# A decayed linear attention and a two-layer MLP in one kernel: the order of the work rewritten, attention in whole chunks on raw scores, its outputs token-major and turned by DMA

## The chip, the core and the metric

One NeuronCore of a Trainium2 chip. The metric is the device time of one execution in microseconds (us), the median of three runs. The profile beside it is of one execution; its span runs from the first to the last recorded instruction.

Names of the engines: PE is the matrix engine (its weight loads are a row of their own, PEld), DVE the vector engine, ACT the scalar engine, POOL the GpSimd engine, SP the sync engine, which here only issues DMAs. Each engine takes its instructions in the order in which the program wrote them for it.

## What is computed

```python
B, H, S, D = 4, 8, 768, 64; block = 64
for b in range(S // block):                          # q, k, v, per head h with decay lam[h]
    intra = (q_b k_b^T * lam^(i-j) for i >= j) v_b
    inter = (q_b * lam^(i+1)) state
    out_b = intra + inter
    state = lam^block * state + (k_b * lam^(block-1-j))^T v_b
x = out as [B * S, H * D]                            # 3072 tokens x 512
h = x @ w_in                                         # 512 x 2048
g = h * tanh(softplus(h))                            # Mish
return g @ w_out                                     # 2048 x 512, f32
```

Both kernels take chunks of 128 positions instead of blocks of 64, which gives the same sums, and compute in float16 with float32 accumulation.

## The kernel before, in words

The sequence is cut into six groups n = 0 to 5. A group is 128 positions of all four batches, so four chunks (n, b) of 128 tokens by 8 heads; its x has 512 tokens. The work of a group has three parts.

**Attention**, before: half a chunk (four heads, two pairs of heads) at a time. `att_a` (L306, once for every half) makes q and k feature-major. For group 1 PE does it, for groups 2 to 5 a DMA transpose on SP's queue (`turn`, L263 to L268). DVE multiplies q by a table of decays (`qT`, L318 or L341), k has been multiplied by its decay before (`scale_k`, L256). Each pair's two heads are copied apart into a zero-padded tile (`kz`, L322 on DVE or L344 on ACT), so that one matmul of 128 rows gives one head's scores. `att_s` (L353) makes four 128x128 score matmuls, and DVE multiplies them by the causal mask (`sb`, L362). `att_o` (L365) adds the state's part and the scores' part, feature-major, so that the result is x as the first layer wants it (L375, L379), and ACT copies it out (`xt`, L382). `att_kv` (L276) and `att_w` (L290) make the new state (matmuls `pv` L283, `raw` L298 on DVE, `w` L299 on POOL).

**First layer**: 16 units of 128 features, each four matmuls of 512 columns into a PSUM bank `ph` and one Mish on ACT into `hsg` (L420, L434).

**Second layer**: for group 0 plain, 64 matmuls of 512 columns (`po`, L442). For groups 1 to 5 as the seven products of a 2x2 block scheme (`fast_unit` L593, `product` L518), each 16 matmuls of 256 columns; DVE makes the sums of the operands (`gsum` L498 per group, `tsum` L479 once) and the combinations of the results.

The order is written out by hand: at group n PE runs the 16 units and the 14 half products of group n, and the attention pieces of group n+1 are let in after given units (`room`, L661 to L667). Loads of q, k and v are issued from POOL's queue, 128 KB each, weights before them (L124 to L143). Outputs leave from SP's and ACT's queues.

Of the kernel before, what the change touches and what calls it, by code (L numbers as in the profile page):

```python
# [20 lines left out]
def kernel(  # L21
# [10 lines left out]
    nc = tc.nc  # L32
# [10 lines left out]
    NVB = 8  # L43
    NKB = 4
    NT = 2
# [3 lines left out]
    loads = ctx.enter_context(tc.tile_pool(name="loads", bufs=NVB))  # L49
    work = ctx.enter_context(tc.tile_pool(name="work", bufs=2))  # L50
    ps = ctx.enter_context(tc.tile_pool(name="ps", bufs=1, space=bass.MemoryType.PSUM))


    kn = [None] * (NG * B)
    qn = [None] * (NG * B)

    vz = [const.tile([128, H, 2 * D], F16, name=f"vz{i}") for i in range(NVB)]

    def chunk_rows(t, i):
        n, b = divmod(i, B)  # L60
        return t[b, :, n * C : (n + 1) * C, :].rearrange("h p c -> p h c")

    def load_k(i):
        if i == 0:
            kn[i] = const.tile([128, H, D], F32, name="kn0")
            nc.sync.dma_start(out=kn[i], in_=chunk_rows(k, i))
            return
        kn[i] = loads.tile([128, H, D], F16, name="kn", tag="kn")
        nc.gpsimd.dma_start(out=kn[i], in_=chunk_rows(k, i))  # L69

    def load_q(i):
        if i == 0:
            qn[i] = const.tile([128, H, D], F32, name="qn0")
            nc.scalar.dma_start(out=qn[i], in_=chunk_rows(q, i))
            return
        qn[i] = loads.tile([128, H, D], F16, name="qn", tag="qn")
        nc.gpsimd.dma_start(out=qn[i], in_=chunk_rows(q, i))  # L77

    def load_v(i):
        nc.gpsimd.dma_start(out=vz[i % NVB][:, :, 0:D], in_=chunk_rows(v, i))  # L80

    WS = 4

    cuts = (0, 128, 256, DF // WS)
    win0 = [const.tile([128, NKC, b_ - a_], F16, name=f"win0{a_}") for a_, b_ in zip(cuts, cuts[1:])]
    win = [None] + [const.tile([128, NKC, DF // WS], F16, name=f"win{s}") for s in range(1, WS)]
    wout = [const.tile([128, NKI // WS, DMO], F16, name=f"wout{s}") for s in range(WS)]

    def load_win(s):
        w = DF // WS  # L90
        if s == 0:
            for t, a_, b_ in zip(win0, cuts, cuts[1:]):
                nc.gpsimd.dma_start(
                    out=t, in_=moe_w_in[:, a_:b_].rearrange("(k p) f -> p k f", p=128))
            return
        nc.gpsimd.dma_start(
            out=win[s],
            in_=moe_w_in[:, s * w : (s + 1) * w].rearrange("(k p) f -> p k f", p=128),
        )

    def load_wout(s):
        w = DF // WS
        nc.gpsimd.dma_start(
            out=wout[s],
            in_=moe_w_out[s * w : (s + 1) * w, :].rearrange("(k p) f -> p k f", p=128),
        )

    def load_chunk(i):
        load_k(i)
        load_q(i)  # L110
        load_v(i)
# [4 lines left out]
    rel = const.tile([128, C], F32, name="rel")  # L116
    maskT = const.tile([128, C], F32, name="maskT")
    gone = const.tile([128, C], F32, name="gone")
    ei = const.tile([128, C], F32, name="ei")
    k0 = const.tile([128, H, D], F16, name="k0")  # L120
    q0 = const.tile([128, H, D], F16, name="q0")
    ek = const.tile([128, 1], F32, name="ek")

    load_k(0)  # L124
    load_q(0)
    nc.scalar.preload_act_table_set("natural_log_exp_and_others")
    load_k(1)
    nc.gpsimd.iota(rel, pattern=[[1, C]], base=0, channel_multiplier=-1,
                   allow_small_or_imprecise_dtypes=True)
    for f, i in ((load_q, 1), (load_v, 0), (load_k, 2), (load_q, 2)):  # L130
        f(i)
    nc.gpsimd.iota(ek, pattern=[[0, 1]], base=MID, channel_multiplier=-1,
                   allow_small_or_imprecise_dtypes=True)
    for f, i in ((load_v, 1), (load_k, 3), (load_q, 3), (load_v, 2), (load_v, 3)):
        f(i)
    for s in range(WS):
        load_win(s)
    for s in range(WS):
        load_wout(s)
    nc.gpsimd.iota(ei, pattern=[[1, C]], base=-MID, channel_multiplier=0,  # L140
                   allow_small_or_imprecise_dtypes=True)
    for i in range(B, 2 * B):
        load_chunk(i)  # L143
# [609 lines left out]
```

## Time and profile before

| | |
|---|---|
| median of three runs | 219.91 us (219.43 to 221.17) |
| profiled execution, span | 217.4 us |
| PE busy | 204.8 us, 94% |
| DVE busy | 146.1 us, 67% |
| POOL busy | 116.6 us, 54% |
| ACT busy | 101.3 us, 47% |
| granted PE clock | full, in every slice |
| HBM | 27.26 MB read, 6.29 MB written |

PE's busy time in the page ends a matmul where its result is out; the next one starts well before that, so that the time a matmul keeps PE from the next one is read from the distance between starts. The medians of the runs lie 2.5 us over the span: what lies around the recorded instructions.

### The profile page before, as it was taken

Reading aid. Unit: us, or ns where it says so; the run is one execution under the profiler, and the core shown is the slowest. Engines: PE = TensorE matmul, PEld = TensorE weight load, DVE = VectorE, ACT = ScalarE, POOL = GpSimd, SP = SyncE. Lnnn points to the kernel's source line nnn. Section 1 sums busy time; section 2 is a strip of 40 time slices with the busy share of each in tenths; the row PEclk is TensorE's granted clock in tenths of the full one; section 3 lists DMA queues with packets and bytes.
Section 4 is the critical chain, followed back from the end, with each engine's and each line's share of the span. In section 5 each row is a group of like instructions: output and inputs, shape, how many; then the busy total and the mean of one; then the engine's idle time right before and its main releaser. Section 6 shows DMA issues by size and latency. Waiting matters only on the chain.

```text
span 217.4 us, 4272 instructions
## 1 busy us (share of the span) xinstructions
PE 204.8 (94%) x1672; PEld 136.6 (63%) x1672; DVE 146.1 (67%) x309; ACT 101.3 (47%) x190; POOL 116.6 (54%) x139
## 2 busy tenths in 40 slices
PE   7899999999999799999979999979999999999993
PEld 2465544576545587745669845669845699644893
DVE  6667561877669999339999419999439987213433
ACT  5465566567665231166522176623166632266410
POOL 7996334998988768808757908757700002000020
PEclk9999999999999999999999999999999999999999
DMA  9999999999999999975999965999985201300014
GB/s 133 141 158 198 203 203 175 175 152 125 150 149 104 100 75 121 163 152 70 104 71 113 142 160 74 119 75 71 151 168 100 48 3 48 130 18 0 0 59 137
DMA packets 103766, 24.66 MB, mean 113 GB/s; under 512 B 93890, under 2 KB 103234, under 8 KB 103746
## 3 DMA queue, kind: packets, MB, share of 16 engines
q0 software_dynamic: 78080, 13.37, 80.3%
q1 hardware_dynamic: 22688, 8.39, 17.8%
q10 hardware_dynamic: 2978, 2.62, 4.0%
q8 instruction: 13, 0.21, 0.4%
q14 instruction: 7, 0.06, 0.1%
HBM read 27.26 MB, written 6.29 MB: 154 GB/s over the span
## 4 chain that ended last, share of the span: by engine, by line
PE 63%; DVE 20%; POOL 5%; issue 4%; DMA 4%; ACT 1%; ACTq 0%; POOLq 0%; DVEq 0%
PE ph L420 26%; PE z L525 10%; PE po L442 6%; PE y L525 6%; PE x L525 5%; DVE qT L318 5%; DVE kz L322 4%; DVE sb L362 4%; DVE gsum L498 4%; DMA win<-in_moe_w_in_dram 4%; PE pO L379 3%; DVE raw L298 3%; PE pS L358 2%; PE fin L525 2%; POOL vz L80 2%
## 5 line engine op out<-in xcount | busy, mean ns | idle before, releaser
L420 PE MATMUL ph<-xt,win 128*128 128x512 f16 (+2 forms) x404 | 89.6, 368 | 0.5 <-ACT hsg L434 0.2
L434 ACT ACTIVATE hsg<-ph 128x512 f16<-128x512 f32 x96 | 57.0, 597 | 45.6 <-PE ph L420 45.5
L420 PEld LDWEIGHTS <-win 128*128 128x128 f16 x404 | 37.0, 98 | 35.1 <-issue 0.6
L299 POOL TENSOR_TENSOR w<-raw,lbm 128x256 f16<-128x256 f32 x32 | 25.2, 791 | 29.0 <-DVE raw L298 28.9
L578 POOL TENSOR_TENSOR u<-u,p 128x512 f32<-128x512 f32 x5 | 6.5, 1293 | 52.0 <-DVE u L576 52.0
L525 PEld LDWEIGHTS <-gsum 128*128 128x128 f16 x336 | 30.8, 98 | 3.5 <-issue 0.5
L362 DVE TENSOR_TENSOR sb<-pS,maskT 128x512 f16<-128x512 f32 x40 | 27.2, 683 | 2.0 <-PE pS L358 1.9
L382 ACT ACTIVATE xt<-pO 128x256 f16<-128x256 f32 x40 | 15.2, 382 | 27.4 <-PE pO L379 27.2
L318 DVE TENSOR_TENSOR qT<-qraw,lq 128x256 f16<-128x256 f16 x32 | 19.1, 598 | 10.3 <-DMA qraw<-qn 10.3
L525 PEld LDWEIGHTS <-hsg 128*128 128x128 f16 x240 | 22.7, 98 | 2.5
L69 POOL DMA_DIRECT2D kn<-in_k_dram x23 | 21.4, 932 | 4.5 <-DMA win<-in_moe_w_in_dram 1.7
L80 POOL DMA_DIRECT2D vz<-in_v_dram x24 | 21.7, 906 | 3.3 <-DMA wout<-in_moe_w_out_dram 1.7
L77 POOL DMA_DIRECT2D qn<-in_q_dram x23 | 20.7, 898 | 5.1 <-DMA wout<-in_moe_w_out_dram 3.3
L498 DVE TENSOR_TENSOR gsum<-hsg 128x1024 f16<-128x1024 f16 x20 | 14.5, 725 | 12.9 <-ACT hsg L434 12.9
L322 DVE COPY kz<-kraw 64x256 f16<-64x256 f16 x64 | 19.9, 311 | 1.9 <-DMA kraw<-ktil 0.9
L379 PE MATMUL pO<-sb,vz 128*128 128x128 f16 x160 | 17.3, 219 | 3.6 <-DVE sb L362 3.2
L525 PE MATMUL z<-tsum,gsum 128*128 128x256 f16 x160 | 20.4, 272 | 0.2
L525 PE MATMUL x<-wout,hsg 128*128 128x256 f16 x160 | 20.1, 273 | 0.0
L358 PE MATMUL pS<-qT,kz 128*128 128x128 f16 x160 | 16.6, 220 | 1.8 <-DVE kz L322 1.6
L358 PEld LDWEIGHTS <-kz 128*128 128x128 f16 x160 | 11.8, 98 | 7.8 <-DVE kz L322 3.0
L298 DVE TENSOR_TENSOR raw<-pv,w 128x256 f32<-128x256 f32 x32 | 13.5, 422 | 4.1 <-PE pv L283 3.4
L379 PEld LDWEIGHTS <-vz 128*128 128x128 f16 x160 | 12.6, 98 | 5.7 <-issue 4.9
(89 smaller groups left out, 242.8 us busy)
## 6 DMA issues: line engine op xcount, KB each, us to landing
out_dram<-osum SPq DMA_DIRECT2D x14, 256.0 KB, 3.2
vz<-in_v_dram POOLq DMA_DIRECT2D x24, 128.0 KB, 4.7
kn<-in_k_dram POOLq DMA_DIRECT2D x23, 128.0 KB, 4.4
qn<-in_q_dram POOLq DMA_DIRECT2D x23, 128.0 KB, 4.6
wout<-in_moe_w_out_dram POOLq DMA_DIRECT2D x4, 512.0 KB, 16.5
win<-in_moe_w_in_dram POOLq DMA_DIRECT2D x3, 512.0 KB, 10.1
out_dram<-osum ACTq DMA_DIRECT2D x5, 256.0 KB, 4.0
out_dram<-osb ACTq DMA_DIRECT2D x4, 256.0 KB, 5.5
```

The costliest lines, as they stand in the source:

```text
L69: nc.gpsimd.dma_start(out=kn[i], in_=chunk_rows(k, i))
L80: nc.gpsimd.dma_start(out=vz[i % NVB][:, :, 0:D], in_=chunk_rows(v, i))
L299: nc.gpsimd.tensor_tensor(out=w_new, in0=raw, in1=lb, op=ALU.mult)
L318: nc.vector.tensor_tensor(out=s.qT, in0=qraw[i][:, 2 * hf : 2 * hf + 2, :], in1=lqh, op=ALU.mult)
L322: nc.vector.tensor_copy(s.kz[rs, :, hp, :], kraw[i][rs, 2 * hf : 2 * hf + 2, :])
L358: nc.tensor.matmul(psS[:, 2 * p + hp, :], s.kz[:, p, hp, :], s.qT[:, p, :], start=True, stop=True,)
L362: nc.vector.tensor_tensor(out=s.sb, in0=psS, in1=bc(maskT, 1, 4), op=ALU.mult)
L379: nc.tensor.matmul(psO[:, p, :], vf[:, o : o + 128], s.sb[:, 2 * p + hp, :], start=False, stop=(hp == 1))
L420: nc.tensor.matmul(ph_t[ni][:, lo:hi], win0[min(ni, 2)][:, kc, max(ni - 2, 0) * 128 : max(ni - 2, 0) * 128 + 128] if ni < w else win[ni // ...
L434: nc.scalar.activation(hsg[n][:, ni, :], ph_t.pop(ni), AF.Mish)
L498: nc.vector.tensor_tensor(out=gsum[n, i][:, ks, :], in0=a, in1=b, op=op)
L525: nc.tensor.matmul(t, lhs(kk, b), rhs(kk, c, c + w), start=(fresh and kk == 0 and (alone or i == 0)), stop=(kk == HK - 1), skip_group_chec ...
```

## The change

The kernel is written anew around the same parts. What it does:

- **Scores**: a whole chunk at a time. q and k are transposed raw and not scaled. A head's scores come from 64 rows of both, without the zero-padded copies: 8 matmuls of 64 rows by 128 columns, even heads into bank `be`, odd ones into `bo`. DVE multiplies each bank by the mask that carries the key's decay (`sb`, L247).
- **Outputs**: token-major. Four matmuls q by state (128 columns) and eight `sb` by v (64 columns) into bank `bz` (L263, L268). DVE multiplies by the query's decay (`xn`, L271), and a DMA transpose on SP writes `xt` (L274). Two chunks of group 1 are turned by PE instead (`later`, L280).
- **State**: one step a chunk instead of two (L289, L297, L298).
- **Transposes of q and k**: for groups 2 to 5 in pairs of chunks, 128x1024 (L230); groups 0 and 1 on PE.
- **Second layer**: group 0 also by the seven products, in the order 1, 2, 6, 5, 7, 3, 4 through two banks G and H. After product 1 ACT copies G to H (L440), product 2 goes on in G, 6 and 7 and 4 in H.
- **Order**: group 0's first layer holds group 1's attention; group 1's first layer follows in halves of 256 columns (`two_units`) with the rest of it and a part of group 2's; then group 0's second layer with the rest of group 2's attention; then, for n = 1 to 4, group n's second layer, group n+1's first layer and group n+2's attention in turns; at the end group 5's second layer by itself.
- **Loads** of q, k, v in pairs of chunks (256 KB); weights between them, the second layer's after the first pair of group 2. All outputs leave from SP.

```diff
-    NVB = 8
-    NKB = 4
-    NT = 2
...
+    def turn_dma(n, bp):
+        for t, to in (("k", kT), ("q", qT)):
+            tile_ = work.tile([128, 2 * JP, C], F16, name=f"{t}T", tag=f"{t}T", bufs=2)
+            nc.sync.dma_start_transpose(out=tile_, in_=pairs[t, n, bp].rearrange("p h c -> p (h c)"))
...
+    def decay_k(n, b, eng):
+        kd[n, b] = work.tile([128, H, D], F16, name="kd", tag="kd", bufs=3)
+        eng.tensor_tensor(out=kd[n, b], in0=kn[n, b], in1=bc(lk, 2, D), op=ALU.mult)
+    def scores(n, b):
+        p_ = [bank(t, [JP, C]) for t in "eo"]
+        for j in range(JP):
+            for t in range(2):
+                rs = slice(64 * t, 64 * t + 64)
+                nc.tensor.matmul(p_[t][:, j, :], kT[n, b][rs, j, :], qT[n, b][rs, j, :],
+                                 start=True, stop=True)
+        for t in range(2):
+            sb[n, b, t] = work.tile([128, JP, C], F16, name="sb", tag="sb", bufs=4)
+            nc.vector.tensor_tensor(out=sb[n, b, t], in0=p_[t], in1=dm[:, t], op=ALU.mult)
...
+    def outputs(n, b, turn=None):
+        po = bank("z", [H, D])
...
+        for j in range(JP):
+            for t in range(2):
+                nc.tensor.matmul(po[:, 2 * j + t, :], sb[n, b, t][:, j, :], vn[n, b][:, 2 * j + t, 0:D],
+                                 start=False, stop=True, skip_group_check=True)
+        xn = work.tile([128, H, D], F16, name="xn", tag="xn", bufs=2)
+        nc.vector.tensor_tensor(out=xn, in0=po, in1=bc(lq, 2, D), op=ALU.mult)
+        dst = x_tile(n)[:, :, b * C : (b + 1) * C]
+        if turn is None:
+            nc.sync.dma_start_transpose(out=dst, in_=xn.rearrange("p h c -> p (h c)"))
+            return None
...
+    def state(n, b, tag, eng):
+        pv = bank(tag, [JP, 128])
+        for j in range(JP):
+            nc.tensor.matmul(
+                pv[:, j, :].rearrange("p (a e) -> p a e", a=2), flat(kd[n, b], j),
+                vn[n, b][:, 2 * j : 2 * j + 2, 0:D], start=True, stop=True)
...
+            raw = work.tile([128, JP, 128], F32, name="raw", tag="raw", bufs=2)
+            nc.vector.tensor_tensor(out=raw, in0=pv, in1=wst[n, b], op=ALU.add)
+            eng.tensor_tensor(out=w_new, in0=raw, in1=lbm, op=ALU.mult)
+        wst[n + 1, b] = w_new
...
+    def two_units(n, ni, r):
+        t = bank(next_bank(), [2, HC])
+        cs = slice(r * HC, r * HC + HC)
+        for u in range(2):
+            for kc in range(NKC):
+                m = (ni + u) % 4 * 128
+                nc.tensor.matmul(
+                    t[:, u, :], win[ni // 4][:, kc, m : m + 128], xt[n][:, kc, cs],
+                    start=(u == 0 and kc == 0), stop=(kc == NKC - 1), skip_group_check=True)
+        nc.scalar.activation(h_tile(n)[:, ni : ni + 2, cs], t, AF.Mish)
...
-    def mm2_unit(n, b, part):
...
-    def fast_unit(n, step, blk):
...
+        def half(p, blk):
+            if blk == 0 and p in (1, 5, 3):
+                m.g = bank("G", [2, HN])
+            t = m.g if p in (1, 2, 5, 3) else m.h
+            product(n, p, t[:, blk, :], blk, p in (1, 5, 3) and blk == 0)
+            if blk == 0:
+                return
+            if p == 1:
+                m.h = bank("H", [2, HN])
+                nc.scalar.activation(m.h, m.g, AF.Copy)
+            elif p == 2:
+                o = osum()
+                nc.scalar.activation(o, m.g, AF.Copy)
+                store(n, 0, 0, o)
+            elif p == 5:
+                m.p5 = work.tile([128, 2, HN], F32, name="r5", tag="r5", bufs=1)
+                nc.scalar.activation(m.p5, m.g, AF.Copy)
+                m.u4 = work.tile([128, 2, HN], F32, name="u4", tag="u4", bufs=1)
+                nc.vector.tensor_tensor(out=m.u4, in0=m.h, in1=m.p5, op=ALU.add)
+            elif p == 7:
+                o = osum()
+                nc.vector.tensor_tensor(out=o, in0=m.h, in1=m.p5, op=ALU.add)
+                store(n, 1, 1, o)
+            elif p == 3:
+                o = osum()
+                nc.vector.tensor_tensor(out=o, in0=m.g, in1=m.u4, op=ALU.add)
+                store(n, 0, 1, o)
+            elif p == 4:
+                o = osum()
+                nc.scalar.activation(o, m.h, AF.Copy)
+                store(n, 1, 0, o)
+        return [(lambda p=p, blk=blk: half(p, blk)) for p in (1, 2, 6, 5, 7, 3, 4) for blk in range(2)]
...
-    for n in range(NG):
-        units = [(mm1_unit, (n, ni)) for ni in range(NKI)]
...
+    first_units(2)
+    first_state(0, "e")
+    first_units(3)
+    first_state(1, "o")
+    for bp in range(2):
+        for t in "kqv":
+            load_pair(t, 2, bp)
+        if bp == 0:
+            for s in range(WS):
+                load_wout(s)
+    first_units(8)
+    first_state(2, "e")
+    first_units(9)
+    first_state(3, "o")
+    first_units(10, 11)
+    turn1(0)
+    decay_k(1, 0, nc.vector)
+    sums(0, 0, 2, 0)
+    first_units(4)
+    scores(1, 0)
+    turn1(1)
+    first_units(5)
+    decay_k(1, 1, nc.vector)
+    first_units(6)
+    outputs(1, 0)
+    state(1, 0, "e", nc.vector)
+    first_units(7)
+    scores(1, 1)
+    sums(0, 0, 1, 3)
+    first_units(12, 13)
+    outputs(1, 1)
+    state(1, 1, "e", nc.vector)
+    turn1(2)
+    first_units(14)
+    scores(1, 2)
+    turn1(3)
+    first_units(15)
+    decay_k(1, 2, nc.vector)
...
+    halves = dense2(0)
...
+    h(1)
+    attended(2, 1)
+    for t, bp in (("k", 0), ("q", 0), ("v", 0)):
+        load_pair(t, 3, bp)
+    for i in range(2):
+        weight_sum(3, i)
+    h(3)
+    attend(2, 2, nc.gpsimd)
+    h(3)
+    attended(2, 2)
+    sums(1, 0, 0, 1)
+    h(1)
+    attend(2, 3, nc.gpsimd)
+    turn_dma(3, 0)
+    h(3)
+    attended(2, 3)
+    for t, bp in (("k", 1), ("q", 1), ("v", 1)):
+        load_pair(t, 3, bp)
+    sums(1, 0, 2, 3)
+    h(3)
...
+    for n in range(1, NG - 1):
...
+        h(3)
+        u(0)
+        s_(0)
+        if m < NG:
+            turn_dma(m, 1)
+        sums(n, 1, 0, 1)
+        u(1)
+        h(1)
+        u(2)
+        o_(0)
+        fetch(("k", 0), ("q", 0))
+        u(3)
+        h(1)
+        u(8)
+        s_(1)
+        sums(n, 1, 2, 3)
+        h(1)
+        u(9, 10)
+        o_(1)
+        fetch(("v", 0), ("k", 1))
+        h(1)
+        u(11)
+        h(1)
+        u(4)
+        s_(2)
+        if m + 1 < NG:
+            turn_dma(m + 1, 0)
+        u(5)
+        h(1)
+        u(6)
+        o_(2)
+        fetch(("q", 1), ("v", 1))
+        h(1)
+        sums(n + 1, 0, 0, 1)
+        h(1)
+        u(7)
+        h(1)
+        u(12)
+        s_(3)
+        sums(n + 1, 0, 2, 3)
+        h(1)
+        u(13)
+        h(1)
+        o_(3)
+        u(14, 15)
+    sums(NG - 1, 1, 2, 0, 1, 3)
+    dense2_alone(NG - 1)
```

In the order's lines `h(m)` writes the next m half products of the second layer, `u` a unit of group n+1, `s_(b)` a chunk's decayed k and scores, `o_(b)` its outputs and state (`attend` and `attended` do the same for group 2), `sums` operand sums on DVE, `fetch` loads.

How this moves instructions on two engines. First DVE during group 1's attention; before, this stood under group 0's second layer. `raw` and `w` are the state, `qT` and `kd` the operands, `sb` the masked scores.

```order
L479 TENSOR_TENSOR tsum_201<-wout_85,wout_83 128x1024
L341 TENSOR_TENSOR qT<-pq,lq 128x256
L298 TENSOR_TENSOR raw<-pv,w_184 128x256
L341 TENSOR_TENSOR qT<-pq,lq 128x256
L298 TENSOR_TENSOR raw<-pv,w_186 128x256
L362 TENSOR_TENSOR sb<-pS,maskT 128x512
```

With the change DVE has the following there, under group 0's first layer.

```order
L225 COPY qT<-bz 128x512
L236 TENSOR_TENSOR kd<-kn,lk 128x512
L384 TENSOR_TENSOR gsum_474<-hsg 128x1024
L384 TENSOR_TENSOR gsum_476<-hsg 128x1024
L247 TENSOR_TENSOR sb<-be,dm 128x512
L247 TENSOR_TENSOR sb<-bo,dm 128x512
L225 COPY qT<-bz 128x512
L236 TENSOR_TENSOR kd<-kn,lk 128x512
L271 TENSOR_TENSOR xn<-bz,lq 128x512
L297 TENSOR_TENSOR raw<-be,w_383 128x512
L298 TENSOR_TENSOR w_383<-raw,lbm 128x512
```

The operand sums of group 0's second layer, the decay of k and the state's product with `lbm` (before on POOL) now stand in this queue ahead of and between the steps that PE's attention waits for.

Second, ACT at the start of a group's second layer. Before (group 2), products 1 and 7 are copied out of two banks that are written in turns, with the attention's copies between.

```order
L568 ACTIVATE p_1693<-x 128x512
L382 ACTIVATE xt<-pO 128x2x128
L570 ACTIVATE p_1729<-z 128x512
L382 ACTIVATE xt<-pO 128x2x128
L573 ACTIVATE osum<-x 128x512
L553 DMA out_dram<-osum 128x2x256
```

With the change (group 1), the copy from G to H is the one that product 2, the next on PE, waits for before it may add to G.

```order
L440 ACTIVATE bH<-bG 128x512
L320 ACTIVATE hsg<-bC 128x512
L320 ACTIVATE hsg<-bA 128x512
L443 ACTIVATE osum<-bG 128x512
L320 ACTIVATE hsg<-bB 128x512
```

The attention's copies and the DMA of the output are gone from ACT; the copy into H is new.

SP's queue, not shown row by row, takes in the loop outputs of group n, the transposes of `xn` of group n+2 and those of k and q pairs in turns. A kT row there waits for the load of its pair, and the rows behind it wait with it.

More of the change, by code (lines that the diff above doesn't have):

```diff
@@ L86, with bank @@
[L86 to L95 removed]
+    def bank(tag, shape, dtype=F32):
+        return ps.tile([128] + shape, dtype, name=f"b{tag}", tag=f"b{tag}")
@@ L158, in busy @@
     def busy(m):
[L160 removed]
+        t = bank("H", [4 * C])
         for _ in range(m):
@@ new lines, with attend @@
+    two_units(1, 0, 0)
+    later = outputs(1, 2, "G")
+    state(1, 2, "e", nc.vector)
+    two_units(1, 2, 0)
+    scores(1, 3)
+    decay_k(1, 3, nc.vector)
+    later()
+    two_units(1, 4, 0)
+    two_units(1, 6, 0)
+    later = outputs(1, 3, "G")
+    state(1, 3, "e", nc.vector)
+    two_units(1, 8, 0)
+    sums(0, 1, 2, 0)
+    later()
+    turn_dma(2, 0)
+    for ni in (10, 12, 14):
+        two_units(1, ni, 0)
+    sums(0, 1, 1, 3)
+    two_units(1, 0, 1)
+    two_units(1, 2, 1)
+    def attend(n, b, kd_eng):
+        decay_k(n, b, kd_eng)
+        scores(n, b)
```

731 lines of the change are left out of this document (279 added, 452 removed).

## The prediction

> **What bounds the kernel now.** I read the page's first section and its chain, then the granted clock, then the chain in order of time, to find where PE waits.
>
> ```profile
> span 217.4 us, 4272 instructions
> PE 204.8 (94%) x1672; PEld 136.6 (63%) x1672; DVE 146.1 (67%) x309; ACT 101.3 (47%) x190; POOL 116.6 (54%) x139
> PEclk9999999999999999999999999999999999999999
> PE 63%; DVE 20%; POOL 5%; issue 4%; DMA 4%; ACT 1%; ACTq 0%; POOLq 0%; DVEq 0%
> ```
>
> PE bounds it at full clock, and DVE is the engine it waits for: 20% of the chain. The chain in order of time has the stages, and the pace of each kind of matmul:
>
> ```profile
> 19.77 0.28 PE L283 MATMUL pv<-vz,ktil 128*128 128x128 f16 x2
> ...
> 55.45 0.89 PE ph L420 x8
> 56.36 0.61 ACT hsg L434
> 57.01 6.20 PE ph L420 x28
> ...
> 90.65 6.04 PE ph L420 x28
> ...
> 124.05 6.04 PE ph L420 x28
> ...
> 157.46 7.77 PE ph L420 x36
> ...
> 165.23 0.22 PE pS L358 x4
> ...
> 187.97 13.81 PE ph L420 x64
> 201.78 1.75 PE x L525 x16
> ...
> 212.28 1.78 PE fin L525 x24
> 214.08 0.29 DVE osum L562
> ```
>
> A matmul of 512 columns takes 13.81/64 = 0.216 us, one of 256 columns 1.75/16 = 0.109, one of 128 columns 0.22/4 = 0.056. With these a group's 16 units are 13.8, its seven products 12.2. The stage from 157.46 to 187.97 (30.5 us) holds those and 80 matmuls of 128 columns (4.5): 30.5, so no wait. The stages from 90.65 and from 124.05 are 33.4 long and hold 96 such matmuls (5.4): 31.4, so 2.0 of waiting each. From 18.9 (group 0's unit 2, one unit before the row at 19.77) to 90.65 are 71.75 us for what the program writes there, 184 x 0.216 + 112 x 0.109 + 240 x 0.056 = 65.3: 6.4 waiting. Together **10.4 us of waits** behind the start; the end behind the last product (about 3.3) and the start (to 18.9) are written the same way after the change, so they stay.
>
> **The work of PE.** Three terms, then what is added.
>
> Group 0's second layer: 64 x 0.216 = 13.8 become 112 x 0.109 = 12.2, **-1.6**.
>
> Scores: eight matmuls of 128 columns per chunk, 0.45 us, become eight of 64 rows. Group 0 already does them so:
>
> ```profile
> 12.81 0.40 PE L230 MATMUL pS<-pqT,pkT 64*128 64x128 f16 x8 [0.31 <-ACT pkT L218]
> 13.14 0.62 PE L244 MATMUL pO<-sb,vz 128*128 128x128 f16 x8
> ...
> 15.14 0.38 PE L162 MATMUL busy<-kzero 128*128 128x512 f16 x1
> 15.45 0.40 PE L230 MATMUL pS<-pqT,pkT 64*128 64x128 f16 x8
> ```
>
> A last matmul shows about 0.22 us, so the eight starts of a group lie within 0.40 - 0.22 = 0.18 us: two run side by side, 0.22 for eight. But the way in and out costs. The 512 columns at 15.14 would free PE after 0.216; the scores start after 0.31, 0.09 late, with no wait shown on the row. The rows at 13.14 start 0.33 after the scores' start where 0.24 would do: another 0.09. So a chunk's scores take 0.22 + 0.18 = 0.40, and 20 chunks save **-0.9**, not 4.5.
> [...]
>
> Outputs: the eight matmuls of `sb` by v go from 128 to 64 columns. No row has 64 columns on full rows. From above, 0.056 each as for 128 columns (if each weight load, one per matmul, sets the pace), no gain; from below, half, 0.028. The nearest row is the 64-row group: 8 matmuls with 8 weight loads in 0.22, 0.028 each, so issuing is no obstacle. I take 0.030: 20 x 8 x 0.026 = **-4.1**; the other end is 0.
> [...]
>
> Added: eight PE transposes (`later`, 0.45) and one dummy matmul (0.22), **+0.7**. The state's matmuls and group 1's transposes are as many as before. Work together: **-5.9**.
>
> **Waits that are new.** Durations on the engines that PE waits for:
>
> ```profile
> L362 DVE TENSOR_TENSOR sb<-pS,maskT 128x512 f16<-128x512 f32 x40 | 27.2, 683 | 2.0 <-PE pS L358 1.9
> L322 DVE COPY kz<-kraw 64x256 f16<-64x256 f16 x64 | 19.9, 311 | 1.9 <-DMA kraw<-ktil 0.9
> L318 DVE TENSOR_TENSOR qT<-qraw,lq 128x256 f16<-128x256 f16 x32 | 19.1, 598 | 10.3 <-DMA qraw<-qn 10.3
> L259 DVE TENSOR_TENSOR ktil<-kn,lk 128x512 f16<-128x512 f16 x8 | 5.4, 688 | 6.8 <-DMA kn<-in_k_dram 6.7
> L498 DVE TENSOR_TENSOR gsum<-hsg x20: 681/692/844, 58.7 to 202.4; 128x1024 f16<-128x1024 f16 x20
> L479 DVE TENSOR_TENSOR tsum<-wout 128x1024 f16<-128x1024 f16 x2 | 1.3, 684 | 0.0
> 18.90:55.40 36.50, 36.17 (x276) 20.67 (x274) 22.93 (x53) 23.51 (x46) 23.87 (x29) 1.00 1.50 176
> ```
>
> A DVE pass over 128x512 or 128x1024 is 0.69 us throughout. Over the kernel DVE loses 39 us of `kz` and `qT` and gains 20 `xn` (14): it gets freer. Not in the first third, though. From 18.9 to about 61 PE now runs both first layers of groups 0 and 1, and DVE gets about 55 passes there: 12 `sb`, 8 operand sums, 6 weight sums, 7 `kd`, 4 `w` for group 0 and 4 for group 1 (moved from POOL), 5 `xn`, 5 `raw`, 2 masks, four copies of `qT`: 38 us in 42, 90%, where the last row shows 22.9 in 36.5. Each stands in line before something PE waits for. Following PE's and DVE's queues from 18.9, with the passes above:
>
> - The states of group 0's chunks 1 to 3: each needs a `kd` that stands behind the previous `w`, the first also behind masks and `lbm`: 1.1 + 0.8 + 0.8.
> - Unit 4 needs `win1`, which a pair of group 1 (768 KB) is now ahead of:
>
> ```profile
> 21.39 0.87 POOL L77 DMA_DIRECT2D qn<-in_q_dram  x1 [1.75 <-DMA win<-in_moe_w_in_dram]
> q0 software_dynamic: 7347, 0.93, 243.6%
> q0 software_dynamic: 2451, 2.43, 123.5%
> ```
>
>   The fourth weight DMA lands at 21.3 (the issue that waited for it). The two queue rows are of 36 to 42 and of 20 to 32 us: 128 KB of q, k, v take 0.85 us, 512 KB of weights 2.6. So 21.3 + 6 x 0.85 + 2.6 = 29.0; PE is there at 28.1: 0.8. The other loads land ahead of need.
> - Chunk 0's outputs and the scores of group 1's chunks 1 to 3 and group 2's chunk 1 need a bank that `xn` or `raw` must have read: 0.4 + 0.5 + 0.7 + 0.5 + 0.5. The turn of chunk 2 needs bank z, whose `xn` stands behind two operand sums: 1.1.
> - x of group 1's chunk 1 by DMA, just in time: 0.3.
>
> That is 7.5 us, against 1 to 2 there before. Then group 0's second layer: product 2 behind the copy G to H. The chain's first rows price such a turn: matmuls end 56.34, ACT 0.61, PE on at 57.01. With its results 0.16 late anyway, 0.8 us. Product 7 needs `u4`, which stands behind two operand sums in DVE's queue: 2.0. Scores of chunk 3 and the next product 1 (bank G until DVE's last sum): 0.5 + 0.9. Together 4.2. In the four loops product 2 waits 0.8 each time, with every later PE row behind it; I add 0.2 in three for outputs whose `sb` ends just in time: 3.8. There DVE has about 22 us of passes in 31, and units stand between each product and what needs its sum, so I see no other. **New waits 15.5, old ones 10.4: +5.1.**
>
> Hidden: ACT loses the attention's copies. POOL loses issues (30 loads of pairs for 60) and group 1's products. SP gets longer rows:
>
> ```profile
> L268 SPq DMA_TRANSPOSE qraw<-qn x16: 1188/1219/2151, 50.0 to 167.8; - x16
> DMA to landing us min/median/max: 2.4/3.4/6.0
> out_dram<-osum SPq DMA_DIRECT2D x14, 256.0 KB, 3.2
> ```
>
> 18 transposes of this size and 16 of twice it at 1.2 and an estimated 2.4 us of issue make 60 us in 217. In the loop a transpose is issued 5 us and more ahead of its reader. Where a kT row waits for its load, outputs wait behind it, which nobody waits for, and one x, needed a stage later. Without that cover a late transpose costs up to 6.0 - 3.4 = 2.6 each.
>
> **Sum.** 217.4 - 5.9 + 5.1 = 216.6 span. The runs' median lies 219.9 - 217.4 = 2.5 over the span, so **219.1 us**, 0.4% under before: the gain on PE is given back in the first third.
>
> **Rivals.**
> A, faster: the waits are half what I count, because PE comes later to each place than I have it (each wait removes the next) and ready work lies ahead. For it: the interleaved stage from 157.46 has none at 70% DVE. Against: 90% of DVE in the first third. 15.5 to 8.5: 212.1.
> [...]
> C, slower: a matmul of 64 columns keeps the pace of 128, since it has the same weights to load. Against it the 64-row group. The place is L268; +4.1 gives 223.2. Above 0.035 us each the kernel is no faster than before, above 0.05 measurably slower.
> D, slower: DVE passes between SBUF tiles stretch when POOL works beside them. `qT` shows it: mean 598 ns, while the same size from PSUM takes 424:
>
> ```profile
> L341 DVE TENSOR_TENSOR qT<-pq,lq 128x256 f16<-128x256 f16 x8 | 3.4, 424 | 2.5 <-PE pq L336 2.2 <-PE pv L283 0.2
> ```
>
>   In the first third some 25 passes are of that kind, 17 us; by 1.4 that is +7, less the 4 us that DVE has free there: 222.1 and, with the waits that follow, 224. Against it: POOL mostly issues DMAs there.
>
> **Chances.** Forecast 0.45 with its own range 217.0 to 221.5; A 0.22, B 0.10, C 0.13, D 0.10. About 1% (2.2 us) is what a measurement can tell, the runs before spread from 219.43 to 221.17. Faster (under 217.7): A, B and 0.04 of the forecast, 0.36. Slower (over 222.1): C, D and 0.01, 0.24. Between: 0.40. The range goes down to A's 212.1, nearly, and up past C and to D: 212.8 to 224.0.
>
> **What would show it.** Right: `pO`-like rows of 64 columns starting 0.03 apart; 0.09 before and after each score group; DVE near 90% from 20 to 60 us and PE waiting 7 to 8 us there, for `kd`, `raw`, `xn`; a gap of 0.8 after every product 1, ended by ACT L440; no other gap over 0.3 in the loops; second loop turn about 31 us long. Wrong: PE waits under 4 us before 61 (A); 64-column starts over 0.05 apart (C); DVE means over 0.8 us (D); PE waiting for DMA L230 or L274.

## The result and the profile after

The changed kernel takes 232.1 us (median of 4, 231.98 to 233.42) against 220.53 for the one before, four runs of each: 1.053 times as long, interval 1.0485 to 1.0582. Medians and ranges in this document are of all executions, ratios and their intervals of the undisturbed ones alone. The forecast was 219.1, at most 224.0. The profiled execution spans 230.3 us, where 216.6 was forecast. All of the missing 13.7 us is lost before 95 us and, a little, at the end; the loops between came out as forecast.

First the page of after.

```profile
span 230.3 us, 4273 instructions
PE 201.4 (87%) x1781; PEld 138.9 (60%) x1781; DVE 135.7 (59%) x219; ACT 84.1 (37%) x142; POOL 75.5 (33%) x73
PE   7786798359998839699999899998999989999992
PEclk9999999958999988999999999999999999999999
DMA  9999999999915995999999529999301341002123
PE 70%; DVE 15%; DMA 7%; POOL 3%; issue 2%; ACT 1%; ACTq 0%; DVEq 0%
```

Two things are new against the page of before. The row PEclk has two dips, each just behind a dip of PE, and the chain has 7% DMA. The share of DVE on the chain fell from 20 to 15%. DVE is busy for 18.3 of the 22 us from 20 to 42, and for 28.0 of the 40 from 20 to 60: the "near 90%" that the prediction named as a sign of being right is not there.

The waits of PE in after, longest first (us in total, times, longest):

```profile
PE bB L340 <- DMA xt<-xn: 6.0, 1, 6.0
PE bG L421 <- ACT bH L440: 3.6, 5, 0.7
PE bH L421 <- DVE u L449: 3.5, 1, 3.5
PE bo L289 <- DVE kd L236: 2.9, 2, 2.3
PE bG L421 <- DVE osum L456: 1.4, 1, 1.4
PE bH L151 <- DVE kzero L137: 1.2, 1, 1.2
PE be L289 <- POOL kd L236: 1.1, 1, 1.1
```

The first is group 1's first pair of units, which needs chunk 1's x, turned by DMA. The third is product 7 of group 0's second layer. Counted from where the pace of the matmul before would have ended, the two are 6.15 and 3.70 us; such counts are used below.

The chain of after in order of time around these two waits:

```profile
38.65 0.60 DVE xn L271
39.27 9.44 DMA xt<-xn
48.76 1.89 PE bB L340 x8
51.93 1.69 PE bC L340 x8
54.28 0.87 PE bA L340 x8
...
80.56 1.72 DVE gsum L384
82.34 1.30 issue
83.64 0.69 DVE u L449
84.38 3.47 PE bH L421 x16
87.85 0.87 PE bG L421 x8
```

The transpose takes 9.44 us from issue to landing. Behind it eight matmuls take 1.89 and then 1.69, where eight of the same take 0.87 from 54.28 on. Behind the second wait 16 matmuls take 3.47, twice 1.75. The same by stretches (PE busy, PEld, DVE, ACT, POOL, then the granted clock, DMA share, GB/s):

```profile
42.00:54.00 12.00, 6.01 (x46) 4.03 (x45) 4.39 (x8) 1.85 (x4) 2.60 (x2) 0.72 1.30 186
54.00:72.00 18.00, 17.72 (x201) 15.42 (x200) 15.21 (x23) 9.70 (x17) 3.09 (x2) 1.00 1.49 101
72.00:84.00 12.00, 7.09 (x81) 5.84 (x80) 9.14 (x11) 1.78 (x3) 8.87 (x7) 1.00 1.29 114
84.00:95.00 11.00, 9.21 (x79) 7.42 (x79) 6.97 (x10) 0.60 (x1) 4.42 (x4) 0.84 0.59 84
```

Granted clock 0.72 over 12 us is 6.8 us at half, 0.84 over 11 is 3.4 at half. The clock's records put them at 46.66 to 53.48 and 84.20 to 87.62: PE had stood still from 42.6 and from 80.7. The halves last 6.83 and 3.41 us, and lie 37.55 us apart, 11 times 3.41; all changes of the clock in the records of after, the first at 9.11 us, lie a whole number of times 3.41 us apart. Such a stretch of 3.41 us is called a window here. How long PE stood still ahead of a half window comes out further below.

So much for the first reading. Theory: two waits, a transpose that lands late beside loads, and `u4` behind operand sums that POOL stretches, cost their own length and then the clock. Rivals: DVE has no time left in the first third, so that each wait removed comes back elsewhere; the transposes are slow of themselves; the clock falls for another reason.

The start of a profiled execution varies: the pause of 0.54 us in the outputs of group 0's last chunk begins at 16.7 in after and at 17.1 to 19.2 in the runs below. Places are compared counted from it.

### The profile page after: what moved, and what is told of

It reads as the page before. It is cut to its first block, busy times and chain, and to the rows that moved or that the text cites. A ratio compares the mean times of both kernels' runs of the same rounds, so it can differ in the third digit from the quotient of the medians.

```text
span 230.3 us, 4273 instructions
## 1 busy us (share of the span) xinstructions
PE 201.4 (87%) x1781; PEld 138.9 (60%) x1781; DVE 135.7 (59%) x219; ACT 84.1 (37%) x142; POOL 75.5 (33%) x73
## 3 DMA queue, kind: packets, MB, share of 16 engines
q1 hardware_dynamic: 34416, 13.11, 31.4%
## 4 chain that ended last, share of the span: by engine, by line
PE 70%; DVE 15%; DMA 7%; POOL 3%; issue 2%; ACT 1%; ACTq 0%; DVEq 0%
PE bG L421 15%; PE bH L421 13%; PE bC L314 8%; PE bB L314 8%; PE bA L314 8%; DMA xt<-xn 4%; DVE gsum L384 3%; PE be L243 3%; PE bB L340 2%; DVE sb L247 2%; PE bC L340 2%; PE bz L268 2%; PE bz L263 2%; DMA q<-in_q_dram 2%; PE bA L340 2%
## 5 line engine op out<-in xcount | busy, mean ns | idle before, releaser
L314 PEld LDWEIGHTS <-win 128*128 128x128 f16 x328 | 30.5, 98 | 24.2 <-issue 0.3
L298 POOL TENSOR_TENSOR w<-raw,lbm 128x512 f16<-128x512 f32 x12 | 17.4, 1451 | 69.7 <-DVE raw L297 69.7
L247 DVE TENSOR_TENSOR sb<-be,dm 128x512 f16<-128x512 f32 x24 | 16.5, 688 | 24.8 <-PE bo L243 24.8
L421 PE MATMUL bH<-tsum,gsum 128*128 128x256 f16 x192 | 25.8, 284 | 3.5 <-DVE u L449 3.5
L421 PE MATMUL bG<-wout,hsg 128*128 128x256 f16 x192 | 23.7, 272 | 5.0 <-ACT bH L440 3.6
L314 PE MATMUL bA<-xt,win 128*128 128x512 f16 (+2 forms) x112 | 27.9, 372 | 0.2
L314 PE MATMUL bC<-xt,win 128*128 128x512 f16 x108 | 27.7, 379 | 0.0
L314 PE MATMUL bB<-xt,win 128*128 128x512 f16 (+2 forms) x108 | 26.9, 371 | 0.0
L271 DVE TENSOR_TENSOR xn<-bz,lq 128x512 f16<-128x512 f32 x20 | 13.8, 691 | 20.8 <-PE bz L268 20.7
L320 ACT ACTIVATE hsg<-bA 128x512 f16<-128x512 f32 x27 | 16.1, 597 | 25.9 <-PE bA L314 25.9
L320 ACT ACTIVATE hsg<-bC 128x512 f16<-128x512 f32 x27 | 16.1, 597 | 25.5 <-PE bC L314 25.5
L247 DVE TENSOR_TENSOR sb<-bo,dm 128x512 f16<-128x512 f32 x24 | 16.3, 680 | 0.0
## 6 DMA issues: line engine op xcount, KB each, us to landing
wout<-in_moe_w_out_dram POOLq DMA_DIRECT2D x4, 512.0 KB, 18.9
```

Source lines behind the costliest of these rows:

```text
L247: nc.vector.tensor_tensor(out=sb[n, b, t], in0=p_[t], in1=dm[:, t], op=ALU.mult)
L271: nc.vector.tensor_tensor(out=xn, in0=po, in1=bc(lq, 2, D), op=ALU.mult)
L298: eng.tensor_tensor(out=w_new, in0=raw, in1=lbm, op=ALU.mult)
L314: nc.tensor.matmul(open_[n, ni][:, lo:hi], win[ni // 4][:, kc, (ni % 4) * 128 : (ni % 4) * 128 + 128], xt[n][:, kc, lo:hi], start=(opens a ...
L320: nc.scalar.activation(h_tile(n)[:, ni, :], open_.pop((n, ni)), AF.Mish)
L421: nc.tensor.matmul(t, lhs(kk, blk), rhs(kk)[:, lo:hi], start=(fresh and kk == 0), stop=(kk == HK - 1), skip_group_check=True)
```

## The experiments

**x of chunks 0 and 1 turned by PE.**

```diff
-    outputs(1, 0)
+    later = outputs(1, 0, "G")
...
     first_units(7)
+    later()
...
-    outputs(1, 1)
+    later = outputs(1, 1, "G")
     state(1, 1, "e", nc.vector)
-    turn1(2)
     first_units(14)
+    later()
+    turn1(2)
```

> x of group 1's chunks 0 and 1 is turned by PE and copied by ACT, as chunks 2 and 3 are; nothing else changes. Theory (the transposes by DMA come late, and PE's clock halves behind that wait): the 6.15 us before the first pair of units of group 1 fall under 1, the granted clock stays 1.00 there (another 2.3), eight transposes more on PE cost 0.45: 230.3 goes to about 222.5. Rival (DVE has no time left in this third, so the wait only moves to the next thing that DVE owes, xn, raw or kd): span over 227, with new waits for DVE of 3 us or more between 42 and 62. Rival (the half clock has nothing to do with the wait): 224.5 and a clock near 0.8 still in that stretch.

Measured: 227.2 us (225.96 to 227.95), span 225.1. Stretches of this kernel, to be set beside those of after:

```profile
42.00:54.00 12.00, 11.58 (x138) 9.95 (x139) 10.33 (x18) 6.97 (x13) 0.83 (x1) 1.00 1.27 181
54.00:72.00 18.00, 16.01 (x180) 13.50 (x179) 13.42 (x19) 6.13 (x11) 7.91 (x6) 1.00 1.19 107
```

PE is busy 11.6 of 12 us where it was 6.0, at full clock, and DVE does 10.3 us there instead of 4.4: it had time. The rival of the full DVE falls. The gain is 4.9 us at the median, less than the 8 worked out. Counted from the pause at the start, the second layer begins 7.9 us earlier, of which 1.5 belong to a shorter wait of the first state: 6.4 for x. A second transpose took 1.2 of the place: the scores of group 2's chunk 0 now come before their q has landed.

```profile
56.32 0.21 PE L243 MATMUL be<-qT,kT 64*128 64x128 f16 x1 [1.04 <-DMA qT<-qn]
```

**Fewer weights, and the weights first.** Two runs on what makes the transposes late.

```diff
-            for s in range(WS):
-                load_wout(s)
+            load_wout(0)
```

> Only the first quarter of the second layer's weights is loaded and stands for all four, so the output's values are wrong and 1.5 MB of loads behind 29 us are gone. Theory (the transposes of x are late because the weights' loads share the 16 DMA engines with them): they land within 4 us, the wait of 6.15 falls under 1 and the half clock behind it goes: about 222. Rival (the transposes are slow by themselves or by one another, four of them within 10 us on SP): landing stays near 9 us, wait and time as after.

```diff
+        if bp == 0:
+            for s in range(WS):
+                load_wout(s)
         for t in "kqv":
             load_pair(t, 2, bp)
-        if bp == 0:
-            for s in range(WS):
-                load_wout(s)
```

> The loads of the second layer's weights are issued ahead of the first pair of group 2's k, q, v; so the two transposes of group 2's k and q, which need that pair, are issued some 8 us later and are no longer beside those of x. Rival to the loads (transposes of 256 KB behind it on SP's queue hold up that of x): x of chunk 1 lands within 4 us, the wait falls to about 1, time 222 or a little more. Theory (loads): x still lands 8 us or more after its issue, and the wait stays over 4.

Measured: 231.03 and 231.51 us; the wait for x is 4.36 and 4.68 instead of 6.15, and the packets of chunk 1's x end 6.9 and 7.5 us after its issue, against 8.6 in after. Two loads changed places and x was late in both. The first run's theory (landing within 4 us) failed; that of the second held, with x landing 8 us after its issue and a wait over 4. Both intervals overlap that of after, so neither run shows a gain. The second run clears the transposes of k and q: they were issued 9 us later and x was late all the same. In the first run the pairs of k, q, v moved into the place of the weights. In a stretch where transposes of k and q and loads run together the queues' packets show what each moved; first after, 46 to 52 us, with weights on the loads' queue:

```profile
q0 software_dynamic: 948, 0.94, 92.1%
q1 hardware_dynamic: 952, 0.24, 30.4%
```

then the run with one quarter of the weights, 48 to 52 us, with pairs of k, q, v:

```profile
q0 software_dynamic: 1654, 0.21, 80.1%
q1 hardware_dynamic: 1663, 0.42, 80.1%
```

In these two stretches it is one packet for one packet: the transposes' packets of 256 bytes move at the pace of the loads' packets, 159 per us beside weights (1 KB), 416 per us beside pairs (128 bytes). It is not so everywhere: while the 512 packets of chunk 1's x themselves moved, the loads' queue moved 681 in after (43.5 to 47.9 us) and 1687 in the run with one quarter of the weights (45.4 to 47.7). That packets of loads move among those of x is thus shown, by which rule the queues take turns is not. That leaves the test without any load beside them.

**A quiet stretch.**

```diff
-    for bp in range(2):
-        for t in "kqv":
-            load_pair(t, 2, bp)
-        if bp == 0:
-            for s in range(WS):
-                load_wout(s)
+    load_wout(0)
...
-    state(1, 2, "e", nc.vector)
+    state(1, 2, "e", nc.gpsimd)
+    for bp in range(2):
+        for t in "kqv":
+            load_pair(t, 2, bp)
```

> One quarter of the second layer's weights stands for all four (the output's values are wrong), and both pairs of group 2's k, q, v are loaded only behind the state of group 1's chunk 2, which moves its last product to POOL so that POOL waits there. So no software load lies on the DMA engines from about 33 to 48 us. The two runs before only changed which loads lay there, and x landed as late. Theory (any software load ahead on the engines holds a transpose back: first packet 4.4 us after the issue against 1.2 in the loops, and 3.6 to 4.4 us of moving against 0.8): both transposes of x land 1.9 us after their issue, the wait of 6.15 falls to at most 1, and PE's clock does not halve. Rival (the first transposes of a kernel are slow, or SP's issue is): landing 7 us or more as before.

Measured: 236.39 us once. The transposes of `xt` between 34 and 42 us, first in after, then in this kernel:

```profile
DMA to landing us min/median/max: 8.5/9.0/9.4
```

```profile
DMA to landing us min/median/max: 2.4/3.1/3.8
```

The packets of chunk 1's x end 1.94 us after the issue, and PE has no wait there. The whole is slower, as loads that come so late make group 2's scores wait 9.8 us for q; what is shown is the cause. Without loads beside it chunk 1's transpose of 128 KB lands in 2.4 us, beside them in 9.4. In after, 3.6 us more lie in the moving of chunk 1's packets (4.4 us against 0.8), with the loads' 681 among them; 3 us more lie ahead of the first packet (1.2 us after the issue without loads, 4.2 with), and why is open.

**PE kept busy in the wait.**

```diff
+    busy(28)
     two_units(1, 0, 0)
```

> 28 matmuls of zeros, 6.05 us, stand ahead of group 1's first pair of units, where PE waits 6.15 for x: PE is busy in the wait, and x lands when it does. Theory (the granted clock halves because PE is idle there): granted clock 1.00 from 42 to 62, the pairs at 0.109 a matmul, some 2.3 us less: 229.8 against 232.1 median. Rival (the clock falls for another reason, or its fall costs nothing since DVE is the limit there): time as after, within 0.5, or the half clock stays.

Measured: 230.97 us (230.41 to 232.02). The stretch with the same wait for x:

```profile
42.00:54.00 12.00, 11.72 (x96) 7.21 (x97) 5.30 (x9) 3.12 (x6) 0.81 (x1) 1.00 1.32 181
```

The clock stays at 1.00 where after has 0.72, so it was PE's standing still that halved it there; the other rival falls. Counted from the pause at the start, the second layer begins 3.45 us earlier than in after, of which 1.47 belong to a shorter wait of the first state: 2.0 for the clock. The medians show 1.1, and the intervals overlap (1.0404 to 1.0514 against 1.0485 to 1.0582). The clock's price there is thus 1 to 2 us, its cause shown and its size less sure.

**Operand sums behind u4.**

```diff
-    sums(1, 0, 0, 1)
     h(1)
+    sums(1, 0, 0, 1)
     attend(2, 3, nc.gpsimd)
```

> In group 0's second layer the two operand sums of group 1 stand behind u4 in the program instead of ahead of it. Theory (product 7 waits because u4 stands behind them in DVE's queue, 0.69 each alone and 1.71 and 1.42 as POOL works beside them): the 3.70 before product 7 fall under 0.7, the half clock behind (14 products at 0.21 instead of 0.11, 1.5) goes: about 225.5. Rival (the sums are needed so soon that what is late moves to products 3 and 4, which need sums or the next product 1): 228 to 230.

Measured: 229.09 us (229.01 to 229.15), 3.0 under after, span 227.2. Product 7 waits 1.20 instead of 3.70, and no half clock follows (15 of its matmuls take 1.80 us, where 16 took 3.47); 1.2 is the copy of product 5 and `u4` themselves, with only one chunk's scores to cover them. The queue was the cause of that wait. The expectation's 225.5, 230.3 less what should go, is missed by 1.7 as a span: 1.2 stays, and chunk 3's outputs now wait 0.5 for their `sb`. The median lies in the rival's 228 to 230, but not for its reason: products 3 and 4 and the next product 1 wait as in after.

**No tensor products of group 2 on POOL.**

```diff
-        state(n, b, "e", nc.gpsimd)
+        state(n, b, "e", nc.vector)
 
-    attend(2, 0, nc.gpsimd)
+    attend(2, 0, nc.vector)
...
```

(the four calls of `attend` alike)

> Group 2's decayed keys and state products go from POOL to VectorE; nothing else changes. Theory (operand sums between SBUF tiles take 1.4 to 1.75 instead of 0.69 whenever a tensor product runs on POOL): all of them 0.69 from 56 to 95, the wait of product 7 falls from 3.70 to 2.0 as forecast, so that no half clock follows it (1.5), the state's wait of 1.24 for POOL's decayed keys goes: some 4 us less, 228 median. Rival (they are stretched by PE's or the DMA's traffic): still 1.4 or more, and the eight passes more on VectorE make it slower than after.

Measured: 230.29 us (229.63 to 232.27). The sums between 56 and 100 us, in after (busy, mean ns of one):

```profile
L365 DVE TENSOR_TENSOR tsum<-wout,tsum 128x1024 f16<-128x1024 f16 x4 | 4.7, 1217 | 0.0
L384 DVE TENSOR_TENSOR gsum<-hsg,gsum 128x1024 f16<-128x1024 f16 x2 | 2.4, 1223 | 0.0
L384 DVE TENSOR_TENSOR gsum<-gsum,hsg 128x1024 f16<-128x1024 f16 x2 | 2.1, 1054 | 0.1
```

and with POOL cleared:

```profile
L365 DVE TENSOR_TENSOR tsum<-wout,tsum 128x1024 f16<-128x1024 f16 x4 | 2.6, 684 | 0.0
L384 DVE TENSOR_TENSOR gsum<-gsum,hsg 128x1024 f16<-128x1024 f16 x3 | 2.1, 692 | 0.1
L384 DVE TENSOR_TENSOR gsum<-hsg,gsum 128x1024 f16<-128x1024 f16 x2 | 1.4, 688 | 0.0
```

Every sum takes 0.69 again. In after, three of the stretched sums, at 80.56, 82.30 and 91.02 us, end 0.55 us behind the end of the POOL product beside them (81.72, 83.17 and 92.22). Product 7 waits 2.42, as the state's product, now on DVE (0.69), stands ahead of its two sums; the state's wait for POOL is gone. But the half clock behind product 7 stays (82.40 to 85.81), so 1.8 us come of the 4 expected, and the intervals touch (1.0377 to 1.0497 here). The rows give the price of POOL's products, 0.7 to 1.1 us on a sum of 0.69; by what they hold the sums up is not shown. As for the clock, 2.42 and 0.45 us of standing still in one window of 3.41 were enough here.

**One edit in the loops.**

```diff
-        h(3)
+        h(2)
         u(0)
+        h(1)
```

> After with one edit: in the four loops the first unit stands between products 1 and 2, so that product 2 no longer waits 0.89 for the copy of the first product's bank. Theory (that wait covers the transpose by DMA of chunk 3's x, which the first unit needs): the unit now waits 0.8 to 2.2 in product 2's place, 232 to 234 median. Rival (the waits add up): 3.5 less, 228.6.

Measured: 233.91 us (231.83 to 235.0): no gain from 3.5 us of waits removed. The waits of PE there:

```profile
PE bB L340 <- DMA xt<-xn: 5.8, 1, 5.8
PE bH L421 <- DVE u L449: 3.5, 1, 3.5
PE bB L314 <- DMA xt<-xn: 2.0, 1, 2.0
PE bG L421 <- DVE osum L456: 1.4, 1, 1.4
```

The third row is new: the first unit, moved ahead, waits for chunk 3's x by DMA. Product 2's wait had covered it. In two of the four loops 2.13 and 1.24 us came back so; for the 1.24 the profile names ACT's copy, which had ended 0.4 us before the unit began, while x had landed 0.1 us before. Behind the 2.13 the clock halved once more, and in this execution the half clock behind product 7 lasted two windows and not one: the mean granted clock is 0.963, some 17 us at half, against 0.978 and 10.2 in after.

**The kernel rebuilt, twice.** First all remedies at once, then with what the first one's trace showed. The second against after, its main edits:

```diff
-        h(3)
-        u(0)
+        h(2)
         s_(0)
+        h(1)
+        u(0)
...
         u(13)
-        h(1)
         o_(3)
+        h(1)
...
-    h(3)
+    for t, bp in (("k", 0), ("q", 0), ("v", 0)):
+        load_pair(t, 3, bp)
+    h(4)
     attended(2, 2)
-    sums(1, 0, 0, 1)
     h(1)
     attend(2, 3, nc.gpsimd)
+    sums(1, 0, 0, 1)
```

beside x of chunks 0 and 1 by PE as above, `mask_decays()` behind group 0's last state, `attended(2, 1)` between products 1 and 2, the scores of group 2's chunk 0 a pair of units later, `sums(1, 0, 2, 3)` behind product 4 and four output tiles.

> All remedies together: x of chunks 0 and 1 turned by PE, masks behind the second state, the scores of group 2's first chunk one pair of units later (its q lands late), in group 0's second layer product 5 done ahead of chunk 2's outputs and the operand sums behind what PE waits for, decayed keys ahead of the loads on POOL, something between products 1 and 2 everywhere, a fourth output tile. Theory: from after's 232.1 go 6.4 (x, measured), 3.0 to 4.5 (sums, with 1.2 of it still waiting in that run), 1.5 (masks), 0.83 x 5 (product 2), 2.4 (state's wait, next product 1), 1.4 (end): 213 median, under the 220 of before. Rival (each wait hides another, of DVE or of a bank): 219 or more.

> The rebuilt kernel again, mended where its trace showed that one wait had covered another: between products 1 and 2 stand the scores and no longer the unit, which waited for chunk 3's x by DMA (0.87, 1.64, 2.15, 0.84); the outputs of chunk 3 are one half product earlier; masks behind the last first state (1.05 of waiting); half of product 7 ahead of the scores of chunk 3, which had waited 2.09 for a bank. Theory (these waits are all that is left between 221.5 and the sum): 5.5 of waits in the loops become about 2.2, 3.1 go in the first half, and the half clock behind 144.6 (1.7) goes: some 8 less, 214 median. Rival (VectorE, or x by DMA, is late by as much at the next place): 219 or more.

Measured: 221.51 us for the first (218.26 to 224.11), ratio to before 0.9968, interval 0.9913 to 1.0023, so no faster than before: the 213 of the sum was far off, and the rival's 219 or more came true. Its trace shows what came back: units waiting 0.87, 1.64, 2.15 and 0.84 between products 1 and 2, the scores of chunk 3 waiting 2.09 for a bank, a state 1.73 behind the masks. The second takes **216.37 us** (215.59 to 218.16), 0.983 times the kernel before, interval 0.979 to 0.987: it is 1 to 2% faster than before, and 2.4 us over the 214 expected. From its page:

```profile
span 214.6 us, 4281 instructions
PE 198.6 (93%) x1789; PEld 137.8 (64%) x1789; DVE 133.4 (62%) x219; ACT 85.1 (40%) x144; POOL 74.7 (35%) x73
PEclk9999999999999999999999999999999999999999
PE 73%; DVE 11%; DMA 9%; ACT 2%; issue 2%; ACTq 0%; DVEq 0%
```

**One remedy taken back.** The second rebuilt kernel, with x of chunks 0 and 1 by DMA again.

> The second rebuilt kernel with one remedy taken back: x of group 1's chunks 0 and 1 goes by DMA again, as in after. Theory (late transposes are the largest term by themselves, whatever else is mended): the wait of about 6 before group 1's first pair is back, with half clock behind it, less the transposes on PE (0.45) and the wait for q of group 2 (1.6) that goes: 216.4 + 6 + 2.2 - 0.45 - 1.6 = 222.5 median. Rival (with the rest mended the waits overlap, so that each is worth little alone): 219 or less.

Measured: 222.7 us (220.55 to 227.03), ratio to before 1.0062, interval 1.0014 to 1.011. PE's first wait in it:

```profile
PE bB L340 <- DMA xt<-xn: 5.6, 1, 5.6
```

The wait is back with its half clock (mean 0.985 against 1.00), 6.3 us in all between the medians against 6.1 worked out. The two kernels ran on different chips; by their ratios to before the difference is 2.3%, or 5.0 us. Either way the two transposes alone turn a kernel that is faster than before into one that is not.

## Why the prediction was wrong

**What held.** A matmul of 64 columns: eight in after take 0.40 us with the last one's latency,

```profile
77.49 0.39 PE L263 MATMUL bz<-w,qT 128*128 128x128 f16 x4
77.71 0.40 PE L268 MATMUL bz<-vn,sb 128*128 128x64 f16 x8
```

and over 160 of them the starts lie 0.029 apart (median; 0.030 forecast). The way in and out of the scores: 0.09 to 0.10 before and after each group in the loops, as forecast; rival B, 215.5 without that cost, falls, and so does C. Product 2 waits 0.83 to 0.89 behind product 1 in all five layers (0.8 forecast). From product 2 to product 2 the loops take 31.4, 31.4 and 30.5 us, the forecast's paces and waits. DVE's passes from PSUM take 0.68.

**The step that failed**, in the prediction's list of new waits, is "x of group 1's chunk 1 by DMA, just in time: 0.3", with its support under Hidden: "Without that cover a late transpose costs up to 6.0 - 3.4 = 2.6 each". The landing of 2.4/3.4/6.0 was that of transposes which ran from 50.0 us on, behind the opening loads. The change puts two at 34.8 and 39.3, among 3.5 MB of loads, where one lands after 9 us, and 6.15 us of waiting stand where 0.3 was forecast. The sign that the prediction named for its being wrong, PE waiting for the DMA of L274, is the first row of the waits; none of the four rivals gave it a price or a chance.

**What was not priced at all** is the clock. The prediction read PEclk as full and kept it so. Each of the two long waits of after cost its length and half of the 4.7 or 3.2 us of matmuls at half clock behind it.

How long was too long, the traces tell together. Cut after from 9.11 us on into windows of 3.41 us, counted from the clock's records, and add up in each the time that PE stood still. Ahead of the last product, two windows at full clock, from 43.24 and 80.79 us, had 3.41 of it, and both were followed by one at half; none of the others had more than 1.92, and none was. In the window from 46.66, at half, PE stood still for 2.11 more, and the next was at half too; in those from 50.07 and 84.20 for 0.07 and 0.17, and the next was at full clock. In other runs a half window followed 2.15 and 2.13 us in one window (each one single wait for x by DMA, in the first rebuilt kernel and in the edited loops); whether a sharp bound lies between 1.92 and 2.13 is not shown. How a wait fell on the windows made a difference: the 2.51 us of the first state in after lay across two, and no half followed; the 2.13 lay inside one; and the same wait of 3.70 cost one half window in after and two in the edited loops.

The span against its forecast, place by place:

| place | forecast | measured | us more |
|---|---|---|---|
| x of chunk 1 by DMA | 0.3 | 6.15 | 5.9 |
| matmuls at half clock, 48.76 to 53.48 | 0 | half of 4.7 | 2.3 |
| product 7 behind u4 | 2.0 | 3.70 | 1.7 |
| matmuls at half clock, 84.38 to 87.62 | 0 | half of 3.2 | 1.6 |
| states of group 0 (1.1 + .8 + .8) | 2.7 | 2.51 + .68 + .68 | 1.2 |
| state of group 2 behind POOL's kd | 0 | 1.24 | 1.2 |
| product 1 of the first loop behind osum | 0.9 | 1.58 | 0.7 |
| banks and the turn of chunk 2 | 3.7 | 3.0 | -0.7 |
| unit 4 for its weights; scores of chunk 3 | 1.3 | 0.1 | -1.2 |
| an output tile not yet stored, at the end | 0 | 0.9 | 0.9 |

These make 13.6 of 13.7. A row is what PE lost at that place, and not what its removal brings: the first two make 8.2, and without those transposes 4.9 were gained at the median. Between 18.9 and 61 us the waits other than x add up to about 6.9 where 7.2 was forecast, by luck: the states are 1.2 over, the banks and unit 4 under. The 0.9 is what the last part gains with a fourth output tile in the second rebuilt kernel. Each execution, before and after, takes 1.7 to 1.9 over its own span; the prediction's 2.5 set the median beside the span of a faster execution. So 219.1 + 13.7 - 0.7 = 232.1.

**Product 7's wait** was foreseen with its mechanism and mis-sized: two sums of 0.69 were counted, and they took 1.71 and 1.42.

```profile
80.56 1.71 DVE L384 TENSOR_TENSOR gsum<-hsg 128x1024 f16<-128x1024 f16 x1 [0.18 <-PE bG L421]
82.30 1.42 DVE L384 TENSOR_TENSOR gsum<-gsum,hsg 128x1024 f16<-128x1024 f16 x1
83.64 0.68 DVE L449 TENSOR_TENSOR u<-bH,r 128x512 f32<-128x512 f32 x1
```

**Rival D** had this right, VectorE's passes between SBUF tiles stretched by POOL; the run without group 2's products on POOL shows it, with sums of 0.69 us where 1.42 to 1.75 stood. Its objection ("POOL mostly issues DMAs there") may be wrong too: from 18.4 to 20.9 us two stretched rows stand beside issues. No run took the issues away, and `kd` at 17.20 us takes 0.68 beside one, so that part is not shown.

```profile
18.45 1.36 DVE L194 COPY lbm<-lbc 64x256 f32<-64x256 f32 x2
19.82 1.06 DVE L184 TENSOR_SCALAR maskT<-rel 128x128 f32<-128x128 f32 x1
```

The two copies (0.29 the first, 1.06 the second) and the mask (0.38 in the first rebuilt kernel) make the first state wait 2.51 for 1.1. D's price was spread over 25 passes; in truth a few hit passes counted, those with a wait of PE behind them. What D gives of the loss is about 2 us shown (1.7 before product 7, and 0.3 of the 0.7 behind `osum`, 1.24 without POOL's products) and 1.2 in the states of group 0, argued only; most of the rest is the DMA and the clock.

**Rival A** (waits halve because PE comes later) did occur in small: unit 4, the banks and the scores of chunk 3 came out 1.9 us under the forecast.

## What to carry to other kernels

A DMA's time from issue to landing belongs to the stretch in which it was read (here 2.4 us without loads, 9.4 beside them): before one is put on PE's path, count the loads that lie beside it in its new place. A long wait of PE can cost more than itself, as those of 6.15 and 3.70 us did here, with 6.83 and 3.41 us at half clock behind them, so the long ones are cut or filled first. And a wait that is removed shows the one that it covered: work out what stands ready behind it, and let the trace of the rebuilt kernel, not the sum of gains, give the next edit.

## What the runs showed of the hardware

- A transpose of 128 KB from SBUF to SBUF: 2.4 us to landing for chunk 1's x in the quiet stretch, 8.5 to 9.4 in after beside 3.5 MB of software loads. In two stretches the two queues' packets went one for one (948 to 952, 1654 to 1663), while an x moved they did not (681 and 1687 to 512).
- The granted clock of after fell to half for 6.83 us and for 3.41 us, behind two windows of 3.41 us in which PE stood still throughout, and behind none at full clock with 1.92 or less. It came back behind half windows with 0.07 and 0.17 us of standing still, and not with 2.11. With matmuls of zeros in the first of these waits it stayed at 1.00.
- A sum of two 128x1024 f16 tiles in SBUF takes 0.69 us on VectorE with group 2's products off POOL, and 1.42 to 1.75 in after where a tensor product on POOL (1.26 to 1.64 us) runs beside it; three such sums end 0.55 us behind the product.
